# State read-out in one burst with P, and batch 1's softmax behind the copy of P

## The chip, the cores and the metric

One core of one Trainium2 chip. The metric is the device time of one execution in microseconds (us); lower is better. "Span" is the part of it that the profile covers, about 1.8 us shorter. "Granted clock" is the mean share of its full clock that TensorE was given during an execution.

## The reference

Eight batches of a two-way attention between 512 rows of x and 32 rows of state (8 heads of 64), then a two-layer network with GELU on the 544 rows of each batch.

```python
scores = scale * x @ state.T;   a  = softmax(scores);   xread = a @ state
scores2 = scale * state @ x.T;  a2 = softmax(scores2);  sread = a2 @ x      # the state read-out
h = concat([xread, sread]) (heads side by side: 4352 x 512) @ w_in          # 512 x 2048
out = gelu(h) @ w_out                                                       # 2048 x 512
```

## The kernel before

The kernel folds state into w_in: P = blockdiag(state) @ w_in (per batch, four chunks of 512 columns), so that the rows of xread need only hp = P.T @ AT (AT: the transposed softmax), GELU into g, and op = g.T @ w_out. TensorE's stream is written by hand: `M(k)` is one hp tile (two products of 512 columns), `U(u)` four products into one output tile, `pmat` a chunk of P, `sread` the state read-out. The accumulators lie in two pools of four banks: `ps_f` for everything short, `ps_o` for the outputs.

```python
def atr(b):                       # batches 0 and 1: transposes on TensorE
    ...
        if b == 0 and t == 1:
            nc.vector.tensor_copy(out=A.AT[:, 0:2, t, :], in_=ps[:, 0:2, :])
            nc.scalar.copy(out=A.AT[:, 2:4, t, :], in_=ps[:, 2:4, :])

def sread(b):
    sr = ps_f.tile([128, 2, 65], FP32, name="sr", tag="f")
    # 32 products: 128 rows x 32 columns of weights, 65 columns moving
    ...
    nc.vector.reciprocal(out=inv, in_=flat[:, 0:130:129])
    nc.vector.tensor_tensor(out=A.srm, ...)      # normalised read-out

# batch 0 and 1 (excerpt of the straight-line part)
    rearr_ones(1)
    norm(1, 0)                    # softmax of batch 1, VectorE
    norm(1, 1)
    U(6)
    pmat(0, (2,), act=(1,))       # copies: half t=0 on VectorE, half t=1 on ACT
    U(7)
    M(8, 9)                       # needs that chunk of P
    sread(1)
    M(10, 11)
    U(8)
    pmat(0, (3,), act=(1,))
# steady loop, p = 0..7 per batch b:  pmat(b, (2, 3)) at p == 3,
#   sread(b + 1) at p == 5, its transpose at p == 7; last batch: mm1_sr two per p
```

The softmax here doesn't subtract the row's maximum and nothing guards it: scores larger than these inputs give would overflow.

## Time and profile before

| | before |
|---|---|
| time, first chip | 221.61 us median of 3 (221.57 to 221.69) |
| the profiled execution | 220.51 us, span 218.74, granted clock 1.0 |
| TensorE busy | 210.0 us |
| longest wait of TensorE after the start | 2.0 us, at 26 to 28 us |

The page gives busy times per engine; the waits give who waited for whom; the chain follows the last instruction back to what released it, as start, length, what. L453 and so on are source lines of each kernel's own file.

### The profile page before, as it was taken

To read this page: it belongs to the slowest core of one execution; us is meant where nothing else is said; L and a number is where in the kernel's file an instruction comes from. 1 tells how busy PE (TensorE), PEld (TensorE's weight loads), DVE (VectorE), ACT (ScalarE), POOL (GpSimd) and SP (SyncE) were. 2 spreads that over 40 slices of the span, in tenths; PEclk is the share of its full clock that TensorE was granted. 3 is DMA by queue.
4 is the path that set the end of the run, shared out by engine and by line. 5 is a ranking of instruction groups with operands and counts; after the bars stand their busy time and mean duration, and the time that the engine had idled before them with its cause. 6 is when DMAs were issued, how large, how long until landed. Compare 5 with 4: busy or idle time off the path is not lost.

```text
span 218.7 us, 3991 instructions
## 1 busy us (share of the span) xinstructions
PE 210.0 (96%) x1663; PEld 100.2 (46%) x1663; DVE 83.8 (38%) x166; ACT 121.8 (56%) x217; POOL 43.3 (20%) x57
## 2 busy tenths in 40 slices
PE   7789789999999999999999999999999999999993
PEld 6535234444444445444544445444444455565442
DVE  4825733816219230942176025802381204200151
ACT  3744754579494537953774479355944463564000
POOL 7664105800133011600170017000000000000000
PEclk9999999999999999999999999999999999999999
DMA  7999999860564807282726755460042002200044
GB/s 182 179 195 205 207 191 129 229 155 5 56 87 157 181 0 99 99 200 40 95 98 161 82 62 131 125 117 3 27 171 43 3 0 99 99 0 0 14 123 154
DMA packets 38723, 22.98 MB, mean 105 GB/s; under 512 B 21936, under 2 KB 34480, under 8 KB 38704
## 3 DMA queue, kind: packets, MB, share of 16 engines
q0 software_dynamic: 13664, 8.23, 27.2%
q1 hardware_dynamic: 24352, 14.09, 24.6%
q10 hardware_dynamic: 688, 0.39, 0.6%
q8 instruction: 13, 0.21, 0.4%
q14 instruction: 6, 0.05, 0.1%
HBM read 17.30 MB, written 8.91 MB: 120 GB/s over the span
## 4 chain that ended last, share of the span: by engine, by line
PE 89%; DMA 3%; DVE 2%; ACT 2%; POOL 1%; issue 1%; POOLq 0%; DVEq 0%
PE op L453 48%; PE hp L404 25%; PE p_ps L365 4%; PE hps L466 3%; PE ops L478 3%; DMA w_in_bf<-in_moe_w_in_dram 3%; PE opl L431 2%; PE sr L328 1%; PE pt L271 1%; ACT g L411 1%; DVE a L294 1%; DVE cs L291 1%; ACT L278 1%; PE xT_ps L211 0%; POOL xb L77 0%
## 5 line engine op out<-in xcount | busy, mean ns | idle before, releaser
L453 PE MATMUL op<-w_out_bf,g 128*128 128x512 bf16 x496 | 118.6, 379 | 0.1
L411 ACT ACTIVATE g<-hp 128x512 bf16<-128x512 f32 x128 | 67.6, 600 | 46.6 <-PE hp L404 46.3
L453 PEld LDWEIGHTS <-g 128*128 128x128 bf16 x496 | 46.9, 98 | 59.5 <-issue 6.4
L404 PE MATMUL hp<-AT,P 128*128 128x512 bf16 x256 | 64.5, 379 | 2.7 <-DVE P L379 2.0
L404 PEld LDWEIGHTS <-P 128*128 128x128 bf16 x256 | 23.3, 98 | 29.2 <-DVE P L379 2.9
L417 DVE COPY osb<-op 128x512 f32<-128x512 f32 x31 | 20.9, 686 | 33.3 <-PE op L453 33.3
L379 DVE CAST P<-p_ps 128x512 bf16<-128x512 f32 x31 | 20.3, 686 | 30.9 <-PE p_ps L365 30.7
L377 ACT CAST P<-p_ps 128x512 bf16<-128x512 f32 x31 | 17.0, 588 | 24.4 <-PE p_ps L365 21.3
L175 POOL COPY x<-xb 128x1024 bf16<-128x1024 bf16 x12 | 12.2, 1044 | 30.8 <-DMA xb<-in_x_dram 25.9
L186 POOL COPY xo<-xb 128x1024 bf16<-128x1024 bf16 x12 | 12.2, 1056 | 0.0
L294 DVE TENSOR_TENSOR a<-e,ics 128x512 bf16<-128x512 bf16 x14 | 12.0, 859 | 0.5
L627 POOL COPY hold<-P 128x1 bf16<-128x1 bf16 x4 | 0.8, 192 | 53.5 <-DVE P L379 53.5
L338 DVE RECIPROCAL inv<-sr 128x2 f32<-128x2 f32 x8 | 1.4, 170 | 24.7 <-PE sr L328 24.7
L291 DVE TENSOR_REDUCE cs<-e 128x16 f32<-128x512 bf16 x14 | 9.5, 675 | 3.4 <-ACT e L278 3.4
L365 PE MATMUL p_ps<-w_in_bf,sbd 64*32 64x512 bf16 x248 | 10.4, 382 | 0.0
L278 ACT ACT_TABLE_LOAD x7 | 9.0, 1283 | 2.0 <-issue 1.3
L411 ACT ACT_TABLE_LOAD x7 | 9.0, 1283 | 0.1
L442 ACT COPY osb<-opl 128x128 f32<-128x128 f32 x1 | 0.3, 266 | 15.2 <-PE opl L431 15.2
L417 DVE COPY osb<-ops 128x512 f32<-128x512 f32 x2 | 1.4, 692 | 18.2 <-PE ops L478 18.2
L466 PE MATMUL hps<-XSR,w_in_bf 128*128 128x256 bf16 x64 | 8.3, 273 | 0.0
L278 ACT ACTIVATE e<-pt 128x512 bf16<-128x512 f32 x14 | 7.6, 594 | 0.1
L466 PEld LDWEIGHTS <-w_in_bf 128*128 128x128 bf16 x64 | 6.3, 98 | 2.4
(67 smaller groups left out, 110.3 us busy)
## 6 DMA issues: line engine op xcount, KB each, us to landing
out_dram<-osb SPq DMA_DIRECT2D x31, 256.0 KB, 2.4
xb<-in_x_dram POOLq DMA_DIRECT2D x7, 512.0 KB, 5.7
w_in_bf<-in_moe_w_in_dram POOLq DMA_DIRECT2D x8, 256.0 KB, 10.4
w_out_bf<-in_moe_w_out_dram POOLq DMA_DIRECT2D x4, 512.0 KB, 11.5
x0f<-in_x_dram SPq DMA_DIRECT2D x2, 256.0 KB, 3.6
out_dram<-osb SPq DMA_DIRECT2D x8, 64.0 KB, 1.7
x0f<-in_x_dram ACTq DMA_DIRECT2D x1, 256.0 KB, 4.4
st_bf<-in_state_dram POOLq DMA_DIRECT2D x1, 192.0 KB, 13.7
```

The costliest lines, as they stand in the source:

```text
L175: nc.gpsimd.tensor_copy(out=A.x4[:, :, :, 64 * t:64 * t + 64].rearrange("p j c d -> p c j d"), in_=src[:, t],)
L186: eng.tensor_copy(out=A.xo[:, :, c0:, 2 + 64 * t:66 + 64 * t].rearrange("p j c d -> p c j d"), in_=src[:, t, c0:],)
L278: nc.scalar.activation(out=A.e[:, :, 64 * half:64 * half + 64], in_=pt.rearrange("p j t c n -> p (j t) (c n)"), func=AF.Exp, scale=scale,)
L294: nc.vector.tensor_tensor(out=A.a[:, :, hs].rearrange("p g (c n) -> p g c n", n=NS), in0=e4, in1=ics[:, :, :].to_broadcast((128, G, 2, NS) ...
L365: nc.tensor.matmul(ps[t][32 * c:32 * c + 32, :], lhsT=sbd[64 * t:64 * t + 64, b, c, 32 * t:32 * t + 32], rhs=w_in_bf[64 * t:64 * t + 64, c ...
L377: nc.scalar.copy(out=dst, in_=ps[t])
L379: nc.vector.tensor_copy(out=dst, in_=ps[t])
L404: nc.tensor.matmul(hp, lhsT=Ps[b][:, t, m * 128:(m + 1) * 128], rhs=atts[b].AT[:, :, t, :], start=(t == 0), stop=(t == 1),)
L411: nc.scalar.activation(out=gs[b][:, m, :], in_=hp, func=AF.Gelu)
L417: nc.vector.tensor_copy(out=osb, in_=ps)
L453: nc.tensor.matmul(ps, lhsT=gs[b][:, m, j * 128:(j + 1) * 128], rhs=w_out_bf[:, m, :], start=(m == 0), stop=(m == MC - 1),)
L466: nc.tensor.matmul(hp, lhsT=w_in_bf[:, c, m * 128:(m + 1) * 128], rhs=XSR[:, c, :], start=(c == 0), stop=(c == HC - 1),)
```

## The change

Four edits, which the prediction counts as five parts. The copy of batch 0's second transposed softmax goes to ACT in one piece (part 1). Batch 1's softmax (`norm`) goes behind the copy of P's third chunk (part 2). From batch 2 on, the read-out is done just before P's chunks 2 and 3, in the same burst of small products, in a bank of the output pool; it stands in the batch's own pass of the loop and no longer in the pass before (parts 3 and 4). The last batch's state products come four per step in the last four steps (part 5).

```diff
-                nc.vector.tensor_copy(out=A.AT[:, 0:2, t, :], in_=ps[:, 0:2, :])
-                nc.scalar.copy(out=A.AT[:, 2:4, t, :], in_=ps[:, 2:4, :])
+                nc.scalar.copy(out=A.AT[:, :, t, :], in_=ps)
 ...
-        sr = ps_f.tile([128, 2, 65], FP32, name="sr", tag="f")
+        pool, tag = (ps_f, "f") if b < 2 else (ps_o, "op")
+        A.sr = pool.tile([128, 2, 65], FP32, name="sr", tag=tag)
 ...
     rearr_ones(1)
+    U(6)
+    pmat(0, (2,), act=(1,))
     norm(1, 0)
     norm(1, 1)
-    U(6)
-    pmat(0, (2,), act=(1,))
     U(7)
 ...
-            if nb == B:
-                mm1_sr(2 * p)
-                mm1_sr(2 * p + 1)
+            if nb == B and p >= 4:
+                for m in range(4 * p - 16, 4 * p - 12):
+                    mm1_sr(m)
 ...
-                else:
-                    pmat(b, (2, 3), act=(1,))
+            if b > 1 and p == 2:
+                sread(b)
+                pmat(b, (2, 3), act=(1,))
+                sread_out(b)
 ...
-            if p == 5 and nb < B:
-                sread(nb)
-            if p == 7 and nb < B:
-                srt(nb)
+            if p == 3 and b > 1:
+                srt(b)
```

## The prediction

> **What bounds the kernel now.** I read the page first: the shares of the engines and the chain that ended last.
>
> ```profile
> PE 210.0 (96%) x1663; PEld 100.2 (46%) x1663; DVE 83.8 (38%) x166; ACT 121.8 (56%) x217; POOL 43.3 (20%) x57
> ...
> PE 89%; DMA 3%; DVE 2%; ACT 2%; POOL 1%; issue 1%; POOLq 0%; DVEq 0%
> ```
>
> TensorE is the bound: 210.0 of 218.7 us busy, and 89% of the chain is its own work. A change can gain only where TensorE waits or spends time on something other than streaming. Next, the list of waits, kept to TensorE, gives one large wait after the start:
>
> ```profile
> PE hp L404 <- DVE P L379: 2.0, 1, 2.0
> ```
>
> Third, the chain in order of time around it (start, length, what):
>
> ```profile
> 21.41 0.60 ACT g L411
> ...
> 24.95 0.69 DVE a L294
> 25.64 0.61 DVE cs L291
> ...
> 26.63 0.69 DVE a L294
> 27.32 0.61 DVE P L379
> ...
> 27.98 1.04 PE hp L404 x4
> ...
> 29.68 0.30 DVE srm L339
> ...
> 30.02 0.61 PE hp L404 x2
> 30.63 0.65 PE op L453 x3
> ...
> 31.32 0.39 PE op L453
> ```
>
> The reader is to see that TensorE's last product before the hole was issued at 25.57, and that it resumes at 27.98. The copy of P it needs sits on VectorE behind batch 1's softmax (two times sum, reciprocal, multiply, 23.94 to 27.32), although the timeline has P's products done at 24.98. The chain then goes on without the hole being caught up: one product waits for the state read-out's normalisation (29.98), and the second product into the output waits for GELUs until 31.32.
>
> Fourth, the same view in the steady state:
>
> ```profile
> 68.83 1.73 PE op L453 x8
> 70.56 0.56 PE p_ps L365 x16
> 71.12 1.83 PE op L453 x8
> ...
> 74.68 1.73 PE op L453 x8
> 76.40 0.36 PE sr L328 x24
> 76.76 0.97 PE hp L404 x4
> ```
>
> No wait at all, but eight products cost 1.73 us in the middle of a run and 1.83 after a burst of P; four cost 0.86, and 0.97 after a read-out (sr). A small-tile burst costs about 0.1 us more than its pieces show. In the single records, products of 512 columns start 0.216 us apart; entering a burst adds 0.094 to that step (70.182 to 70.492), and leaving it 0.1 (sr's last start 76.567, the next product at 76.692, 0.125 instead of 0.029, and 0.011 on the step after).
>
> **What the Trainium skill says.** "TensorEngine Tiling (Array Packing)", Key Properties: changing the tiling mode drains TensorE, changing only the tile does not. The trace agrees: 0.09 to 0.11 us at every border, also between two small modes: the 128*64 transposes of batch 1 end at 20.252, sr (128*32) starts at 20.402, 0.150 instead of 0.053. "PSUM — Partial Sum Buffer", PSUM bank collisions: two engines may not touch the same bank and partitions at once, so software orders them. The trace agrees: ACT's half of the first AT copy starts at 11.71, right after DVE's half of the same bank (11.39 to 11.67), although the transposes ended at 11.24. "ScalarE: Activation LUTs", What ACT_TABLE_LOAD costs: 1283 ns per load plus a drain of 1380 ns; the trace shows 1.28 us and then the next ACTIVATE 0.02 us later, so no such drain is charged here.
>
> **The change, part by part.**
>
> (1) AT copy of batch 0. Removed: DVE's half and ACT's half in a row. Added: one ACT copy of 128x512 bf16 from PSUM; the same shape took 0.59 us for the first batch's x transpose (6.72). It can start when the transposes end, 11.24 + 0.04 = 11.28, and ends at 11.87, so the second product of hp starts at about 11.92 instead of 12.13. The next four GELUs (2.07 us in the chain) and the products behind them move with it: 0.21 us. No load is in the way: the nearest is xb of batch 1, landed 18.37, used at 19.39.
>
> (2) Batch 1's softmax behind P. Everything here moves up by the 0.21 of (1). P's products end at 24.98 - 0.21 = 24.77; DVE and ACT copy P at once and end about 25.5. TensorE finishes its output products at 25.57 and goes straight on: the 2.0 us wait goes. The next limit is ACT: the copy of P ends at 25.45, the GELU table load takes 1.28 (to 26.75), then four GELUs of 0.515 end at about 28.83. The output product that needs the fourth runs at 28.88 instead of 31.32: **2.44 us** gained up to there, (1) included. The second wait in the chain, one product waiting for the read-out's normalisation, must go as well, or VectorE's new order (P, softmax, then srm at about 28.75 + 0.50 = 29.25) would hold TensorE. The built program of the changed kernel says that it goes: that hp is now in the bank of an earlier hp and waits for ACT; the read-out's bank goes to the transposes of batch 1, which come at about 30.4. From 28.88 on, the sequence to the end is the old one moved. Loads that could stop it: w_in's last piece landed 28.65, needed at 31.64 - 2.44 = 29.20; w_out's last 31.08, needed at 34.8; the transposed x of batch 2 landed 41.48, needed at 45.1. All pass, the first by 0.55 us.
>
> (3) Read-out merged with P, batches 2 to 7: six times. Removed per batch: one entrance into and one exit out of small tiles (0.094 + 0.107 = 0.20). Added: one change from 128*32 to 64*32, which by the 128*64 to 128*32 case costs 0.097. Gain **0.105 us** each, 6 x 0.105 = **0.63 us**. The number of products does not change.
>
> (4) Bank and order. sr takes a bank of the output pool. It is free in time: the first output of the batch before is copied at 64.56 to 65.25, sr would come at about 68 (before's times). The later outputs then need banks whose copies end at 66.1 and 68.7, for use at 68.8 and 69.6. P's third and fourth tile need GELUs done by 67.1, and 0.15 us is the narrowest margin (batch 3, where the table load comes late, 85.66). srm is ready at about 71.0, its transpose comes at 71.4. Cost 0.
>
> (5) The last batch's state products (hps), four per step in the last four steps instead of two in eight: ACT needs 2 x 0.52 + 4 x 0.35 = 2.4 us per step, TensorE 0.86 + 1.75 + at least 0.86 = 3.5. Cost 0.
>
> Sum: 2.44 + 0.63 = 3.07 us. 221.61 - 3.07 = 218.5 us, 1.4% less.
>
> **The rivals.** (a) The small modes 128*32 and 64*32 follow each other without a drain, so that both borders go: then 6 x 0.20 = 1.2 us, sum 3.65, 218.0 us. For it: both use four column groups. Against it: the measured 0.15 us from 128*64 to 128*32, and the skill's sentence. (b) Another wait takes the place of the 2 us. For it: after (2) TensorE is held by ACT (table load plus four GELUs) for about 0.4 us; if ACT's copy of P or the load came later, or if VectorE's srm at 29.25 were in the way after all, 0.4 to 1 us would be given back: about 219.3. Against it: the waits of the built program, and ACT is idle from 24.4 until P. (c) The gain of (2) is eaten later because a load paced it: w_in's last piece has only 0.55 us to spare; if loads slide by a microsecond, 0.5 us is lost, 219.0. (d) The new steady order stalls: sr waits for VectorE's output copies, P for GELUs in batches 2 to 7. Even 0.1 us each is 0.6 us and would eat all of (3): 219.1. Against it: the margins in (4), and the slow multiply on VectorE (1.05 to 1.41 us instead of 0.69 in batches 2 and 3, while GpSimd copies) gets freer, as GpSimd's copy into xo must now wait for the later read-out.
>
> **Range and chances.** Centre 218.5. Up by (b), (c) or (d) to 219.3; down by (a), or somewhat more from (2), to 217.8. For over 2% it must fall under 217.2, 1.3 us more than I can find: (a) alone gives 0.6. Slower would need a stall of over 7 us.
>
> **What the profile after would show.** (1) ACT's AT copy at 11.28, 0.59 long, and the first GELU at about 12.33 instead of 12.54. (2) No wait of hp for DVE P over 0.1 us; a wait for ACT's GELU of 0.3 to 0.5 us in the output products near 28.5; softmax of batch 1 on VectorE from about 25.5 to 28.8. (3) sr and P back to back, with 0.12 to 0.13 us from sr's last start to P's first, a drain; 0.03 would be rival (a). (4) TensorE's span from the first steady batch to the end shorter by 0.6 us and no wait over 0.1 us at sr, P or the outputs. The prediction is wrong if TensorE shows new waits in batches 2 to 7, or if the output product that ran at 31.32 does not come by about 29.

## The result, and the profile after

| | before | after |
|---|---|---|
| time, first chip | 221.59 us median of 4 (221.38 to 221.69) | 217.5 us median of 4 (217.29 to 217.82) |
| ratio | | 0.9818, 95% interval 0.9801 to 0.9835 |
| profiled execution | 220.51, span 218.74 | 217.82, span 216.1 |

A ratio is the mean time of one kernel's fast runs over that of the other's of the same rounds, so not quite the ratio of the medians. The kernel is 1.8% faster. The prediction said 218.5 with 217.8 as its low end: 0.3 us outside the range. The gain was 4.1 us instead of 3.07.

But the spans of the two profiled executions differ by 2.68 us only (218.74 to 216.06). A trace that shows less than the predicted 3.07 us and a timing that shows more cannot be explained by one wrong term.

The page of the changed kernel, engines and chain:

```profile
PE 210.0 (97%) x1663; PEld 101.2 (47%) x1663; DVE 80.1 (37%) x165; ACT 122.3 (57%) x217; POOL 43.5 (20%) x57
...
PE 85%; DMA 11%; POOL 2%; issue 1%; ACT 0%; POOLq 0%
```

TensorE is still busy 210.0 us: nothing that streams was removed. The waits of TensorE, all that the view lists:

```profile
PE warm_ps L132 <- DVE warm L75: 1.0, 1, 1.0
PE p_ps L390 <- DMA w_in_bf<-in_moe_w_in_dram: 0.7, 2, 0.5
PE pc L230 <- DVE xT L216: 0.3, 1, 0.3
PE hp L407 <- DVE AT L311: 0.3, 1, 0.3
```

The 2.0 us wait of hp for DVE's P is gone, and all that is left lies before 12 us. On VectorE the timeline shows P ahead of the softmax (start, length, what):

```profile
24.74 0.69 DVE L382 CAST P<-p_ps 128x512 bf16<-128x512 f32 x1 [1.70 <-PE p_ps L368]
25.35 0.68 DVE L291 TENSOR_REDUCE cs<-e 128x16 f32<-128x512 bf16 x1
...
28.02 0.69 DVE L294 TENSOR_TENSOR a<-e,ics 128x512 bf16<-128x512 bf16 x1
```

What replaced it is a load, which the view of waits doesn't list because one product of the burst had begun and counts as busy. The chain of the changed kernel shows it:

```profile
15.71 13.85 DMA w_in_bf<-in_moe_w_in_dram
29.56 0.04 issue
29.60 0.41 PE p_ps L368 x7
```

The last piece of w_in landed at 29.56 in this execution (28.65 before), while TensorE had begun the burst that needs it at 29.11. That is rival (c) of the prediction, 0.45 us. And the merged burst, in the same view:

```profile
63.69 1.73 PE op L456 x8
65.41 0.36 PE sr L328 x29
65.77 0.56 PE p_ps L368 x16
66.33 1.83 PE op L456 x8
```

One 1.83 instead of a 1.83 and a 0.97. From sr's last start to P's first it is 0.122 or 0.123 us in each of the six batches, where sr's own groups of four follow each other in steps of about 0.03: the change between the two small modes costs time, as predicted (0.12 to 0.13). From the output products behind w_in's last chunk of P to the end, before needs 218.74 - 32.05 = 186.69 us and after 216.06 - 30.01 = 186.05: 0.64 us for the merging, predicted 0.63. (The expectation of merge_only below has 0.60, from the span rounded to 216.1.)

So within the traces the prediction holds, less 0.45 us for a load (2.68 + 0.45 = 3.13 us, predicted 3.07). The open question is where the timed executions of before had their extra 1.1 us.

### The profile page after: what moved, and what is told of

Same layout as the page of the kernel before. It is cut to its first block, busy times and chain, and to the rows that moved or that the text cites. A ratio compares the mean times of both kernels' runs of the same rounds, so it can differ in the third digit from the quotient of the medians.

```text
span 216.1 us, 3993 instructions
## 1 busy us (share of the span) xinstructions
PE 210.0 (97%) x1663; PEld 101.2 (47%) x1663; DVE 80.1 (37%) x165; ACT 122.3 (57%) x217; POOL 43.5 (20%) x57
## 4 chain that ended last, share of the span: by engine, by line
PE 85%; DMA 11%; POOL 2%; issue 1%; ACT 0%; POOLq 0%
PE op L456 47%; PE hp L407 23%; DMA w_in_bf<-in_moe_w_in_dram 11%; PE p_ps L368 4%; PE hps L469 3%; PE ops L481 3%; PE opl L434 2%; PE pt L271 1%; PE sr L328 1%; POOL w_in_bf L89 1%; POOL xb L77 0%; POOL w_out_bf L99 0%; PE aT_ps L307 0%; PE srT L352 0%; PE st_ps L141 0%
## 5 line engine op out<-in xcount | busy, mean ns | idle before, releaser
L407 PEld LDWEIGHTS <-P 128*128 128x128 bf16 x256 | 23.8, 98 | 27.9 <-issue 1.1
L294 DVE TENSOR_TENSOR a<-e,ics 128x512 bf16<-128x512 bf16 x14 | 9.7, 692 | 0.5
L469 PE MATMUL hps<-XSR,w_in_bf 128*128 128x256 bf16 x64 | 7.6, 273 | 0.0
L132 PE MATMUL warm_ps<-warm 128*128 128x128 bf16 x59 | 6.1, 270 | 1.0 <-DVE warm L75 1.0
L481 PE MATMUL ops<-w_out_bf,g_sr 128*128 128x512 bf16 x32 | 7.1, 379 | 0.0
```

Source lines behind the costliest of these rows:

```text
L407: nc.tensor.matmul(hp, lhsT=Ps[b][:, t, m * 128:(m + 1) * 128], rhs=atts[b].AT[:, :, t, :], start=(t == 0), stop=(t == 1),)
L469: nc.tensor.matmul(hp, lhsT=w_in_bf[:, c, m * 128:(m + 1) * 128], rhs=XSR[:, c, :], start=(c == 0), stop=(c == HC - 1),)
L481: nc.tensor.matmul(ps, lhsT=g_sr[:, m, s * 128:(s + 1) * 128], rhs=w_out_bf[:, m, :], start=(m == 0), stop=(m == MC - 1),)
```

## The experiments

**Theory A.** Before's profiled execution was one of a quicker kind. Ordinary ones hold about 1 us more at one place, which the change removes. **Rival B.** The extra time comes from outside (outside the span, or a low clock that comes whatever the kernel does). Eleven runs, of ten kernels, were made on three chips, all correct; before was timed on each chip as well, and each execution's span and granted clock is listed.

**base_again.** The kernel before, no edit.

> The kernel before, unchanged, for a second profile. The first profiled execution of it took 220.51 us (span 218.74), its timed ones 221.4 to 221.7. Theory A (the profiled execution was a lucky one): the timed executions have spans of about 219.8, and a new profile of an ordinary one shows a stretch about 1.1 us longer than the first trace, at one place, before 36 us, where loads and TensorE meet. Rival B (the 1.1 us lies outside the span): spans stay at 218.7 while the times stay at 221.6, so time minus span is 2.9 instead of 1.8. Rival C: no difference, the time falls to 220.5 on this chip.

Measured: 220.42 to 221.45 us, in two groups: 220.42, 220.68, 220.78 with granted clocks of 0.997 to 0.999, and 221.39, 221.44, 221.45 with 0.992. The spans follow (218.7 to 219.0, and 219.6 to 219.7), so the difference is inside the span. (What the first group lacks to 1 lies, in the trace, behind TensorE's work: in this run's profile the clock is at half from 218.47 us on, and the last product starts at 215.43.) Over all three chips, before's 39 executions with a listed clock fall apart in the same way:

| before | executions | mean us | range |
|---|---|---|---|
| granted clock 0.997 or more | 20 | 220.57 | 220.35 to 220.78 |
| granted clock 0.990 to 0.992 | 19 | 221.53 | 221.39 to 221.82 |

The first chip's four timed executions (221.38 to 221.69; no clocks are listed for them) belong to the second kind by their times alone; its profiled one was of the first. The two kinds differ by 0.96 us. (In at_only and merge_only below, which keep the hole, TensorE's wait of 2.0 us before hp, as it is, 3 of 12 executions are of the second kind; with the 19 of 39 above that makes 22 of 51.) The new profile again fell on an execution of the first kind, so this run alone does not show the place.

**at_only.** Part 1 alone.

```diff
-                nc.vector.tensor_copy(out=A.AT[:, 0:2, t, :], in_=ps[:, 0:2, :])
-                nc.scalar.copy(out=A.AT[:, 2:4, t, :], in_=ps[:, 2:4, :])
+                nc.scalar.copy(out=A.AT[:, :, t, :], in_=ps)
```

> Part 1 alone: the second half of batch 0's first transposed softmax copied by ACT in one piece. By the prediction 0.21 us less than before (the trace after has the first GELU 0.21 us earlier against the copy of P it follows). If the 1.1 us that before's timed runs have over its profile comes from the first 13 us, about 1.3 us less.

Measured: 220.42 to 220.52 in five executions (mean 220.46), 221.45 with clock 0.990 in the sixth. Both kinds are still there. Against before's first kind it is 0.11 us, of the size of the spread; that this part saves its 0.21 in timed executions is not settled. (The profiles of base_again and at_only, both with a late start of the full clock, see after_third, have the first GELU at 12.81 and 12.54: 0.27 us, one trace each.)

**norm_only.** Part 2 alone.

```diff
     rearr_ones(1)
-    norm(1, 0)
-    norm(1, 1)
     U(6)
     pmat(0, (2,), act=(1,))
+    norm(1, 0)
+    norm(1, 1)
     U(7)
```

> Part 2 alone: batch 1's softmax behind the copy of P. By the prediction 2.2 us less (2.44 minus the 0.21 of part 1), 1.9 if w_in's last piece lands after 29.2 us. If the missing 1 us belongs to this part, because in ordinary executions of before the softmax chain or the wait behind it is longer than in the profile, 3.2 us less.

Measured: 218.11 to 218.49 (mean 218.28), no clock under 0.998. That is 2.29 us under before's first kind (predicted 2.2), 3.25 under its second. So both readings of the expectation are right, each for one kind; the second kind does not occur here.

**merge_only.** Parts 3 to 5 alone, that is the changed kernel with parts 1 and 2 undone.

```diff
-                nc.scalar.copy(out=A.AT[:, :, t, :], in_=ps)
+                nc.vector.tensor_copy(out=A.AT[:, 0:2, t, :], in_=ps[:, 0:2, :])
+                nc.scalar.copy(out=A.AT[:, 2:4, t, :], in_=ps[:, 2:4, :])
 ...
+    norm(1, 0)
+    norm(1, 1)
     U(6)
     pmat(0, (2,), act=(1,))
-    norm(1, 0)
-    norm(1, 1)
```

> Parts 3 to 5 alone: read-out merged with P in batches 2 to 7, its bank, the order of the state products at the end; parts 1 and 2 undone. By the prediction 0.63 us less (the trace after shows 0.60 over this stretch). If the missing 1 us belongs here (waits in batches 2 to 7 that before's profile did not have), 1.6 us less.

Measured: four executions at 219.72 to 220.04 (mean 219.89, 0.68 us under before's first kind; predicted 0.63), two at 220.85 and 220.98 with clocks of 0.992 and 0.991. This time the profile caught an execution of the second kind. The view by windows (stretch, its length, busy times of PE, PEld, DVE, ACT and POOL, then the granted clock, DMA share, GB/s):

```profile
28.00:29.00 1.00, 1.00 (x26) 0.40 (x28) 0.00 (x0) 0.53 (x2) 0.00 (x0) 0.96 1.25 205
29.00:30.00 1.00, 1.00 (x34) 0.37 (x19) 0.46 (x2) 0.56 (x2) 0.00 (x0) 0.50 1.94 171
30.00:31.00 1.00, 1.00 (x4) 0.39 (x4) 0.00 (x0) 0.60 (x1) 0.00 (x0) 0.50 1.99 175
31.00:32.00 1.00, 0.78 (x3) 0.39 (x3) 0.00 (x0) 0.60 (x1) 0.00 (x0) 0.50 1.56 195
32.00:33.00 1.00, 1.00 (x11) 0.17 (x10) 0.00 (x0) 0.00 (x0) 0.00 (x0) 0.83 1.45 197
33.00:34.00 1.00, 1.00 (x14) 0.53 (x9) 0.69 (x1) 0.59 (x1) 0.00 (x0) 1.00 1.46 202
```

The reader is to see the third number from the end: TensorE runs at half its clock. The clock's record has it from 28.93 to 32.34, 3.41 us, and 3.41 x 0.5 over 219.1 is the missing 0.8% of the mean. The same windows in the first profile of before have 1.00 throughout; for instance:

```profile
30.00:31.00 1.00, 0.97 (x5) 0.41 (x5) 0.00 (x0) 0.88 (x2) 0.00 (x0) 1.00 2.08 170
```

TensorE's timeline of merge_only around it:

```profile
27.83 1.04 PE L408 MATMUL hp<-AT,P 128*128 128x512 bf16 x4 [2.04 <-DVE P L383]
28.80 0.57 PE L329 MATMUL sr<-xo,e 128*32 128x65 bf16 x32
29.30 1.89 PE L408 MATMUL hp<-AT,P 128*128 128x512 bf16 x4
```

The first four hp products after the hole take 1.04 us, the next four 1.89. From the first of them to the next burst of P it is 4.78 us here (27.83 to 32.61) and 3.66 in before's first profile (27.98 to 31.64): 1.12 us, the difference between the kinds within its spread. It is less than half of 3.41, probably because part of the slowed stretch was spent waiting anyway: in before's first profile the eight products of 29.31 to 31.71 already take 1.32 and 1.24 us for four instead of 1.04.

The half clock starts 1.1 us after TensorE's hole of 2.4 us ends. Does the hole cause it?

**warm_hole.** The kernel before with dummy products in the hole; nothing else moves.

```diff
         hp = ps_f.tile([128, S], FP32, name="hp", tag="f")
+        for _ in range(34 if (b, m) == (0, 8) else 0):
+            nc.tensor.matmul(hp[:, 0:128], lhsT=warm, rhs=warm, start=True, stop=True)
         for t in range(2):
```

> The kernel before with 34 dummy products of zeros (128x128, 0.056 us each, 1.9 us) issued into batch 0's ninth hp tile in the hole of TensorE at 26 to 28 us; the softmax stays ahead of the copy of P, so VectorE's chain and the end of the wait do not move. Theory A (the hole itself makes the clock of TensorE fall to half for 3.4 us in some executions, which costs 1.0 us): all executions at 220.4 to 220.8 us, none with a granted clock under 0.996, while before on the same chip still shows both kinds. Rival B (the low clock comes to some executions from outside, whatever TensorE does there): both kinds, 220.5 and 221.5, as before.

Measured: 220.33 to 220.75 (mean 220.47) in six executions, no clock under 0.997; before on the same chip had 5 of 11 at 0.992. Its timeline of TensorE:

```profile
24.73 1.04 PE L455 MATMUL op<-w_out_bf,g 128*128 128x512 bf16 x4
25.61 2.06 PE L404 MATMUL hp<-warm 128*128 128x128 bf16 x34
27.81 1.03 PE L406 MATMUL hp<-AT,P 128*128 128x512 bf16 x4
```

The useful product still comes at 27.81, after the same softmax on VectorE. Products of zeros in front of it do nothing but keep TensorE busy, and the second kind is gone. Rival B would have left both; that it left none of six by luck has, at the rate of 22 in 51, a chance of 1 in 30.

**long_hole.** The other direction: half of the softmax done twice.

```diff
     norm(1, 1)
+    norm(1, 1)
     U(6)
```

> The kernel before with the second half of batch 1's softmax done twice (same result), which lengthens the hole from 2.4 to about 4.0 us. Theory A: every execution has the half clock afterwards (granted clock at most 0.993), time 220.45 + 1.65 + about 1.0 = 223.1 us in all of them. Rival B: both kinds in the mix of before, 222.1 and 223.1 us.

Measured: 223.34 to 224.31 (mean 223.71), all six with clocks of 0.985 to 0.992. The wait is 3.6 us long:

```profile
PE hp L404 <- DVE P L379: 3.6, 1, 3.6
```

and in the profiled execution the clock is at half from 28.02, still inside the hole, for 6.83 us, twice 3.41. The view by windows shows its beginning:

```profile
28.00:30.00 2.00, 0.52 (x2) 0.25 (x3) 1.39 (x3) 0.00 (x0) 0.00 (x0) 0.50 1.39 199
```

With a hole of 4 us, every execution is struck. Two had 0.985 (224.01 and 224.31), which fits two such stretches; the other four, at 0.991 or 0.992, average 223.49, still 0.4 us above the expectation, which is left open.

**after_again.** The changed kernel, no edit.

> The changed kernel unchanged, with before on the same chip, for its executions' clocks. Theory A: no execution under 0.996 in granted clock, because its longest gap between starts of products is 0.49 us; times 217.3 to 217.8, the spread being the landing of w_in's last piece. Rival B: some executions at 0.992, 1 us longer.

Measured: 217.24 to 217.59 (mean 217.34) in four executions, no clock under 0.999. In this profile w_in's last piece landed at 28.25, so the wait of the first profile is missing and what the prediction had put next is seen:

```profile
25.30 1.28 ACT L414
26.60 2.08 ACT g L414 x4
28.67 0.04 issue
28.72 0.39 PE op L456
29.11 0.34 PE p_ps L368 x8
```

The table load, four GELUs, and then the output product that needs the fourth: ACT paces this stretch.

**p_later.** The changed kernel with the last chunk of batch 0's P later, away from w_in's landing.

```diff
     U(8)
-    pmat(0, (3,), act=(1,))
     U(9)
+    pmat(0, (3,), act=(1,))
     atr(1)
```

> The changed kernel with the last chunk of batch 0's P moved behind the next four output products, 0.86 us later. If the 0.4 us that TensorE waits in the trace after for w_in's last piece (landed 29.56, wanted at 29.12) is all that a late landing costs, the executions come at 217.2 to 217.4 without the 217.7 to 217.8 ones, 0.2 us less than the changed kernel on average. If the wait only moves to a later product (the hp that need that chunk come 1.3 us after it), no change.

Measured: 217.25 to 217.67 (mean 217.34), the same as after_again. In neither profile did the load come late, and one execution at 217.67 is left although that wait is out of the way. So this is inconclusive: the 0.45 us wait is shown in one trace, but it isn't what makes all of the executions of 217.6 to 217.8.

**hole_less.** The kernel before with a shorter hole: only the last multiply of the softmax goes behind the copy (sum, reciprocal and multiply of `norm` can be called apart).

```diff
-    norm(1, 1)
+    norm(1, 1, (0,))              # sum and reciprocal
     U(6)
     pmat(0, (2,), act=(1,))
+    norm(1, 1, (1,))              # multiply
```

> The kernel before with only the last multiply of batch 1's softmax moved behind the copy of P: the hole of TensorE between two starts falls from 2.41 to about 1.80 us. In its undisturbed executions 0.61 us less than before's, 219.8. Theory A leaves open how long a hole must be: if 1.8 us is too short, no execution has a granted clock under 0.996; if it is long enough, some have 0.992 and come 1 us later, but fewer than before's 18 of 33.

Measured: 219.57 to 219.94 (mean 219.82) in six executions, no clock under 0.999. (The expectation's 33 counts the first chip by its times.) The hole was 1.63 us between starts, a little shorter than expected:

```profile
PE hp L408 <- DVE P L383: 1.3, 1, 1.3
```

The kernel is 0.75 us faster than before's first kind, which is the hole's shortening (2.41 - 1.63 = 0.78). A hole of 1.63 us was not followed by a half clock in any of six executions; at the rate of 22 in 51, as for 2.41 us, that would be luck of 1 in 30. Taken together and by their listed clocks, 22 of 51 executions with the hole of 2.4 us had the half clock, 6 of 6 with the longer one, and at that place none of 42 with a shorter, filled or removed one (norm_only 5, warm_hole 6, hole_less 6, p_later 5, combo 6, one of which has it elsewhere, the changed kernel 14). Rival B would not follow the hole like this.

What decides between the two kinds is not tested, but the clock's records in the traces give a hint. In all 13 profiles each change of the clock comes a whole number of 3.413 us after the first. In merge_only's, one such step (25.51 to 28.93) holds the whole idle time of TensorE (25.80 to 27.83), and the half clock follows it; in the three undisturbed profiles with the same hole (before, base_again, at_only) a border between two steps (at 27.67, 27.32 and 27.43) falls into the idle time. If that decides, (3.41 - 2.03) / 3.41 = 40% of the executions are struck, an estimate, against 22 of 51. The 1.25 us of idle time in hole_less's profile lay whole in one step (24.03 to 27.44) and nothing followed.

**after_third** and **combo.** The changed kernel again, and a version that goes on from what the profile after shows: ACT's copy of P delays the table load, so both halves are copied by VectorE; batch 1's read-out joins that burst; and the edit of p_later.

```diff
-    pmat(0, (2,), act=(1,))
+    pmat(0, (2,))
+    sread(1)
+    sread_out(1)
     norm(1, 0)
     norm(1, 1)
     U(7)
     M(8, 9)
-    sread(1)
-    sread_out(1)
     M(10, 11)
     U(8)
-    pmat(0, (3,), act=(1,))
     U(9)
+    pmat(0, (3,), act=(1,))
     atr(1)
```

> The changed kernel once more, beside the next one: 217.25 us, now and then 217.6 to 217.8, no granted clock under 0.996.

> The changed kernel, taken further: batch 1's read-out also in the burst with P's chunk, both halves of that chunk copied by VectorE, so that ACT's GELU table load need not wait behind a copy (ready at 25.4 instead of 26.6), and the last chunk of P behind the next four output products. The output product that waits for the fourth GELU should run at about 28.55 instead of 28.72, the later wait for w_in goes: 217.1 us, 0.15 to 0.2 us less than the changed kernel. If VectorE's two copies in a row hold the first hp (wanted at 26.0, second copy done 26.05) longer than that, no gain.

Measured on the same chip: the changed kernel 217.27 to 217.72 (mean 217.53, no clock under 0.997), combo 217.01 to 217.29 in five executions (mean 217.14) and 218.65 in one. Among executions with a clock of 1.0 it is 217.31 (two) and 217.12 (four), 0.19 us apart, as expected, but on few executions. The sixth, which is the profiled one, has a half clock elsewhere, in the loading phase:

```profile
10.00:12.00 2.00, 1.80 (x19) 1.25 (x16) 0.88 (x3) 0.45 (x1) 2.00 (x4) 0.65 1.19 186
12.00:14.00 2.00, 1.91 (x6) 0.50 (x4) 0.53 (x3) 1.44 (x3) 0.90 (x2) 0.50 1.23 178
```

There TensorE had waited 1.0 us for w_in's first piece, beside other gaps, and the clock was at half from 10.59 for 3.41 us. That part of combo is the same as in the changed kernel, so the exposure is probably theirs too; no other profile shows it. The verdict on combo stays open; it is at best 0.1 to 0.2% better.

after_third's profiled execution, at 217.72, also answers what p_later left open. It does not wait for w_in's last piece, but its first GELU comes at 12.65 us instead of 12.17 in after_again (217.25), and the delay stays to the end. The clock's record gives TensorE the full clock from 6.67 us on, in after_again from 4.90. Six dummy products of the start, first after_again, then after_third:

```profile
4.91 0.50 PE L132 MATMUL warm_ps<-warm 128*128 128x128 bf16 x6
5.08 0.85 PE L132 MATMUL warm_ps<-warm 128*128 128x128 bf16 x6
```

So at least two things make executions of 217.6 to 217.8: a late load (the first profile) and a late full clock at the start (this one). The second is read from one pair of traces and was not tested; the listed clocks do not count it, because the records begin with the full clock.

## Why the prediction was wrong, point by point

| term | predicted | measured against before's undisturbed kind (220.57) |
|---|---|---|
| (1) AT copy | 0.21 | in the traces 0.21 (from the start of the second half of P's first chunk to the first GELU: 10.18 to 12.54, against 10.10 to 12.25); timed 0.11, unsettled |
| (2) softmax behind P | 2.23 | 2.29 (norm_only) |
| (3) to (5) merging, bank, end | 0.63 | 0.68 (merge_only), 0.64 in the traces |
| sum | 3.07 | 3.10 (mean of 14 executions of the changed kernel, 217.47) |

**The step that failed** is the line "Sum: 2.44 + 0.63 = 3.07 us. 221.61 - 3.07 = 218.5 us". The 3.07 was read from a trace of an execution of 220.51 us and was taken from the median of executions of another kind. On its own base it gives 220.51 - 3.07 = 217.44, and 217.5 was measured. The step's missing term is the half clock that follows the hole: 0.96 us in the executions that have it, 19 of 39 on three chips, and by their times all the timed ones on the first chip. The change removes the hole and with it this term. The profile of the page could not show it, but two numbers side by side could have raised the question: 220.51 for the profiled execution and 221.57 to 221.69 for the timed ones.

**(1)** The mechanism was right: ACT's copy began with the end of the transposes (11.20) and took 0.58 us.

**(2)** Right in mechanism and size. The output product predicted for 28.88 came at 28.72 in after_again and at 28.79 in the first profile. The second wait, for the read-out's normalisation, is gone as predicted, in norm_only's profile too. The sentence "All pass, the first by 0.55 us" was wrong for the first profiled execution: the piece landed 0.9 us later than before's, and rival (c) took 0.45 us there. In after_again, with 28.25, it passed.

**(3), (4), (5)** Right. The border between the two small modes costs 0.122 us from start to start, so rival (a) is refuted (the prediction's 20.252 is where the last transpose starts, not where it ends; its sum is from starts and holds), and no new wait appears at sr, P or the outputs (rival (d)).

**Rival (b)** did not come true beyond the predicted wait for GELUs.

## What to carry to other kernels

A hole in TensorE's stream can cost more than its length: one of 2.4 us was followed in 22 of 51 executions by 3.4 us at half clock and 1 us of loss, and either shortening it to 1.6 us or filling it with products of zeros removed that. Before a gain read from a trace is subtracted from a timed median, compare the profiled execution's own time and granted clock with the timed ones; where they differ, the trace is of another kind. When small-tile bursts are merged, count the borders that go (here one of the four around the two bursts of a batch, 0.1 us), not the bursts.

## What the Trainium skill lacked or had wrong

- "TensorE: Matmul & The Clock Gate", Why this matters for your kernels: it asks for no idle gaps of TensorE over about 3 us. Here a gap of 2.41 us between starts (2.0 us idle) brought the half clock in 22 of 51 executions, one of about 4.0 us in 6 of 6, one of 1.63 us in none of 6. Part 1 of the page fits the rest: it gives the window as 3413 ns and free-running; the half clock lasted 3.41 us, or 6.83, and the clock's changes come in steps of 3.413 us.
- "TensorEngine Tiling (Array Packing)", Key Properties: says that a change of mode drains, but not what it costs. Here 0.09 to 0.11 us per border, also between 128*32 and 64*32 (0.122 us from start to start instead of 0.03).
- "TensorE: Matmul & The Clock Gate", Back-to-back issue gap: gives about 131 ns per product of 512 columns in a sustained stream with weight loads. The runs of such products in the steady loop here take 216 ns each (eight in 1.73 us).
- "ScalarE: Activation LUTs", What ACT_TABLE_LOAD costs: the load is 1.28 us as stated; the drain of 1380 ns beside it is not seen, the next ACTIVATE starts 0.02 us after the load.
